# A fused window attention and SwiGLU kernel: a written-out order against an order planned over engines, banks and transfers, with groups of 256 tokens and loads without cast

## The chip, the cores and the metric

One core of one Trainium2 chip. The metric is the device time of one execution in microseconds (us). In the profile, PE is TensorE, DVE is VectorE, ACT is ScalarE, POOL is GpSimd, SP is SyncE, whose work here is to issue transfers.

## The reference

Attention with 4 sink positions and a window of 128 over 4 batches, 8 heads, 768 positions and head size 64, then an RMS norm and a gated feed-forward (512 to 1536 to 512) over the 3072 tokens:

```python
scores = (1.0 / np.sqrt(D)) * np.matmul(q, k.transpose(0, 1, 3, 2))
keep = is_sink | in_window            # pos < 4, or 0 <= row - pos < 128
scores = np.where(keep, scores, -1000000000.0)
a = np.exp(scores - np.max(scores, axis=-1, keepdims=True))
a = a / (np.sum(a, axis=-1, keepdims=True) + 1e-09)
x = np.matmul(a, v)                   # then heads side by side: (3072, 512)
...
xn = x / rms * rms_g
g = xn @ w_gate
silu = g * (1.0 / (1.0 + np.exp(-g)))
out = (silu * (xn @ w_val)) @ w_out
```

Inputs and output are float32; the products are in bfloat16.

## The kernel before

**Attention.** A *visit* is one tile of 128 query positions of one batch for four of the eight heads; there are 48 (`n`: batch, tile, half). It takes three steps. `a_unit` makes the scores of the current and the previous 128 keys in PSUM (L264 for the first tile of a batch, L269 otherwise) in one buffer of two banks, `s2`, of which there is one; lets VectorE overlay the masked part (L275, L281) and the sink scores (L285) and take the row maximum (L288); lets ScalarE take four exponentials (L293); and lets GpSimd pack the sink columns (L299). `b_unit` transposes the probabilities on PE (L308, L312), copies them out on ScalarE (L317) and lets GpSimd select the current and the old part (L325, L329). `c_unit` multiplies by V (L341, L348, L353), divides by the sum (L362, L363) and, after both halves of a tile, squares and sums the rows (L370, L372, L376). `d_unit` scales a tile (L384) and transposes it into `xnt` (L389, L392).

**Each batch's Q and K** are loaded by GpSimd with a cast to bfloat16 (L97), reordered and scaled by VectorE (`order_unit`, L190, L194), transposed on PE (`qk_unit`, L204) and copied to `QT` and `KT` (L210, L214, L218). `sink_unit` (L231, L237, L240) makes the sink scores of a half batch, `vs_unit` (L249) lays out the sink rows of V.

**Feed-forward.** A group is three tiles, 384 tokens (`GROUP = 3`), eight groups. `f_unit` makes gate and value for one of twelve slices of 128 of the 1536 columns (L407), tanh (L412) and two products on VectorE (L414, L418). `o_unit` makes the output of one tile from twelve slices (L424), copies it (L429) and stores it from SyncE (L431).

**Loads.** All but the norm's weight are issued by GpSimd with a cast (L97, L106, L126, L174), in this order: Q and K of batch 0, three tiles of V, the first quarter of the gate and value weights, three tiles of V, the other quarters, the output weights; then Q, K and V of the next batch, from the slots below. `fold_w` (L133, L137) multiplies the norm's weight into the loaded weights in place, on VectorE.

**Order.** Steps of visits are put into slots by hand: slot `n` holds `a_unit(n)`, `c_unit(n - 2)`, `b_unit(n - 1)` and every second time a `d_unit`; a batch's loads, reordering and transposes are put 11 to 1 slots ahead of its first visit. Nine slots run first; then `weave` interleaves six slots with each group's feed-forward by nominal costs. The framework's scheduler makes the final order of each engine from it. PSUM: four banks shared by most steps (`b1`), two for `s2`, two for `pv`.

Of the kernel before, what the change touches and what calls it, by code (L numbers as in the profile page):

```python
# [17 lines left out]
NEG = -1.0e30  # L18


@with_exitstack
def kernel(
# [32 lines left out]
    GROUP = 3  # L55
# [4 lines left out]
    NCH = 4  # L60
    CW = DFF // NCH
    FPC = FTN // NCH
# [4 lines left out]
    stage = ctx.enter_context(tc.tile_pool(name="stage", bufs=8))  # L67
    vpool = ctx.enter_context(tc.tile_pool(name="vpool", bufs=B * NT))
    spool = ctx.enter_context(tc.tile_pool(name="spool", bufs=2))
    ppool = ctx.enter_context(tc.tile_pool(name="ppool", bufs=3))  # L70
    xpool = ctx.enter_context(tc.tile_pool(name="xpool", bufs=3))
    small = ctx.enter_context(tc.tile_pool(name="small", bufs=4))
    xtpool = ctx.enter_context(tc.tile_pool(name="xtpool", bufs=3))
    hpool = ctx.enter_context(tc.tile_pool(name="hpool", bufs=FTN + 3))
    fpool = ctx.enter_context(tc.tile_pool(name="fpool", bufs=3))
    opool = ctx.enter_context(tc.tile_pool(name="opool", bufs=3))
    psum = ctx.enter_context(tc.tile_pool(name="psum", bufs=4, space=bass.MemoryType.PSUM))

    ident = const.tile([P, P], BF16, name="ident")
    nc.gpsimd.memset(ident, 0.0)  # L80
    nc.gpsimd.affine_select(
        out=ident, in_=ident, compare_op=ALU.not_equal, fill=1.0,
        base=0, pattern=[[-1, P]], channel_multiplier=1,
    )
    QT = [const.tile([P, HP, S], BF16, name=f"QT{i}") for i in range(2)]
    KT = [const.tile([P, HP, 2, S], BF16, name=f"KT{i}") for i in range(2)]
    PK = [const.tile([P, P], BF16, name=f"PK{i}") for i in range(3)]
    VS = [const.tile([P, 2, 4 * VW], BF16, name=f"VS{i}") for i in range(2)]

    ST = {}  # L90
    SO = {}
    V16 = {}

    def load_qk(b, half):
        for nm, src in (("q", q), ("k", k)):
            st = stage.tile([P, 4, NT * D], BF16, name=f"{nm}st", tag="st")
            nc.gpsimd.dma_start(  # L97
                out=st,
                in_=src[b, 4 * half:4 * half + 4, :, :].rearrange("h (p j) d -> p h (j d)", j=NT),
            )  # L100
            ST[(nm, b, half)] = st

    def load_v(b, t):
        v16 = vpool.tile([P, H, VW], BF16, name="v16", tag="v16")
        nc.vector.memset(v16[:, :, D:D + 1], 1.0)
        nc.gpsimd.dma_start(  # L106
            out=v16[:, :, 0:D],
            in_=v[b, :, t * P:(t + 1) * P, :].rearrange("h t d -> t h d"),
        )
        V16[(b, t)] = v16  # L110

    load_qk(0, 0)
    load_qk(0, 1)
    for t in range(3):
        load_v(0, t)

# [4 lines left out]
    nc.sync.dma_start(out=rmsg, in_=moe_rms_g.rearrange("(kt p) -> p kt", p=P))  # L121

    def load_w(c):
        cols = slice(c * CW, (c + 1) * CW)
        for dst, src in ((wg_bf, moe_w_gate), (wv_bf, moe_w_val)):
            nc.gpsimd.dma_start(  # L126
                out=dst[:, :, cols], in_=src[:, cols].rearrange("(kt p) f -> p kt f", p=P),
            )

    def fold_w(c):  # L130
        cols = slice(c * CW, (c + 1) * CW)
        for kt in range(KTN):
            nc.vector.tensor_scalar(  # L133
                out=wg_bf[:, kt, cols], in0=wg_bf[:, kt, cols],
                scalar1=rmsg[:, kt:kt + 1], scalar2=None, op0=ALU.mult,
            )
            nc.vector.tensor_scalar(  # L137
                out=wv_bf[:, kt, cols], in0=wv_bf[:, kt, cols],
                scalar1=rmsg[:, kt:kt + 1], scalar2=0.5, op0=ALU.mult, op1=ALU.mult,
            )  # L140


    for i in range(2):
        nc.vector.memset(KT[i][64:128, :, 0, :], 0.0)
        nc.vector.memset(KT[i][0:64, :, 1, :], 0.0)
        nc.gpsimd.memset(VS[i], 0.0)
    for i in range(3):
        nc.gpsimd.memset(PK[i], 0.0)
    negbig = const.tile([P, 1], FP32, name="negbig")
    nc.vector.memset(negbig, NEG)  # L150
    nhalf = const.tile([P, 1], FP32, name="nhalf")
    nc.vector.memset(nhalf, -0.5)

    m_old = const.tile([P, P], I16, name="m_old")
    nc.gpsimd.memset(m_old, 1)
    nc.gpsimd.affine_select(
        out=m_old, in_=m_old, compare_op=ALU.is_gt, fill=0,
        base=0, pattern=[[1, P]], channel_multiplier=-1,
    )

    m_first = const.tile([P, P], I16, name="m_first")
    nc.gpsimd.memset(m_first, 1)
    nc.gpsimd.affine_select(
        out=m_first, in_=m_first, compare_op=ALU.is_gt, fill=0,
        base=0, pattern=[[1, P]], channel_multiplier=-1,
    )
    nc.gpsimd.memset(m_first[:, 0:NS], 0)

    for c in range(NCH):
        load_w(c)  # L170
        if c == 0:
            for t in range(3, NT):
                load_v(0, t)
    nc.gpsimd.dma_start(out=wo_bf, in_=moe_w_out.rearrange("(ft p) d -> p ft d", p=P))  # L174

    SINK = {}
    PT = {}
    PS = {}
    PV = {}
    X16 = {}  # L180
    RR = {}
    XNT = {}

    def order_unit(b, half):

        for nm in ("q", "k"):
            so = stage.tile([P, NT, 4, D], BF16, name=f"{nm}so", tag="so", bufs=4)
            src = ST.pop((nm, b, half)).rearrange("p h (j d) -> p j h d", j=NT)
            if nm == "q":
                nc.vector.tensor_scalar(  # L190
                    out=so, in0=src, scalar1=scale, scalar2=None, op0=ALU.mult,
                )
            else:
                nc.vector.tensor_copy(out=so, in_=src)  # L194
            SO[(nm, b, half)] = so

    def qk_unit(b, hp):
        half, hi = divmod(hp, 2)
        par = b % 2
        for nm in ("q", "k"):  # L200
            pt = psum.tile([P, 512], FP32, name="pqk", tag="b1").bitcast(BF16)
            so = SO[(nm, b, half)]
            for j in range(NT):
                nc.tensor.transpose(  # L204
                    out=pt[:, j * P:(j + 1) * P],
                    in_=so[:, j, 2 * hi:2 * hi + 2, :], identity=ident,
                )
            src = pt[:, 0:NT * P].rearrange("c (j p) -> c p j", j=NT)
            if nm == "q":
                nc.scalar.copy(  # L210
                    out=QT[par][:, hp, :].rearrange("c (p j) -> c p j", j=NT), in_=src,
                )
            else:
                nc.vector.tensor_copy(  # L214
                    out=KT[par][0:64, hp, 0, :].rearrange("c (p j) -> c p j", j=NT),
                    in_=src[0:64],
                )
                nc.scalar.copy(  # L218
                    out=KT[par][64:128, hp, 1, :].rearrange("c (p j) -> c p j", j=NT),
                    in_=src[64:128],  # L220
                )

    def sink_unit(b, half):

        par = b % 2
        ps = psum.tile([P, 512], FP32, name="psk", tag="b1")
        for t in range(1, NT):
            for hi in range(2):
                hp = 2 * half + hi
                c0 = (t * 2 + hi) * 2 * NS  # L230
                nc.tensor.matmul(  # L231
                    out=ps[:, c0:c0 + 2 * NS].rearrange("p (h s) -> p h s", s=NS),
                    lhsT=QT[par][:, hp, t * P:(t + 1) * P], rhs=KT[par][:, hp, :, 0:NS],
                    start=True, stop=True,
                )
        sk = spool.tile([P, NT, 4, NS], FP32, name="sk", tag="sk", bufs=4)
        nc.vector.tensor_copy(  # L237
            out=sk[:, 1:NT], in_=ps[:, 4 * NS:NT * 4 * NS].rearrange("p (t h s) -> p t h s", s=NS, h=4),
        )
        nc.gpsimd.affine_select(  # L240
            out=sk[:, 1], in_=sk[:, 1], compare_op=ALU.is_ge, fill=NEG,
            base=0, pattern=[[0, 4], [-1, NS]], channel_multiplier=1,
        )
        SINK[(b, half)] = sk

    def vs_unit(b):

        for hh in range(4):
            nc.gpsimd.tensor_copy(  # L249
                out=VS[b % 2][32 * hh:32 * hh + NS, :, hh * VW:(hh + 1) * VW],  # L250
                in_=V16[(b, 0)][0:NS, :, :].rearrange("p (x h) c -> p x h c", h=4)[:, :, hh, :],
            )

    def a_unit(n):
        bt, half = divmod(n, 2)
        b, t = divmod(bt, NT)
# [276 lines left out]
```

## Time and profile before

| what | value |
|---|---|
| median of 3 runs | 341.91 us (341.86 to 342.92) |
| profiled execution | 341.6 us, its span 339.9 us |
| busy: PE, DVE, ACT, POOL | 278.8, 237.1, 193.9, 127.8 us |
| mean granted clock of PE | 0.925 |
| loads and stores | 43,197 packets, 20.83 MB |
| HBM read, written | 28.31 MB, 6.29 MB |

Busy time is the union of an engine's instructions. Matmuls are pipelined, so a busy PE need not be PE at its full rate: the time from one matmul's start to the next says more than its duration. In a row of the timeline or of the groups the parts are start, duration, engine, line, operation, `out<-in`, sizes and count; what stands in brackets is the idle time of that engine just before, and what ended it. "DMA" in the slices is the mean busy share of the 16 transfer engines in tenths, PEclk the granted clock in tenths.

### The profile page before, as it was taken

To read this page: it belongs to the slowest core of one execution; us is meant where nothing else is said; L and a number is where in the kernel's file an instruction comes from. 1 tells how busy PE (TensorE), PEld (TensorE's weight loads), DVE (VectorE), ACT (ScalarE), POOL (GpSimd) and SP (SyncE) were. 2 spreads that over 40 slices of the span, in tenths; PEclk is the share of its full clock that TensorE was granted. 3 is DMA by queue.
4 is the path that set the end of the run, shared out by engine and by line. 5 is a ranking of instruction groups with operands and counts; after the bars stand their busy time and mean duration, and the time that the engine had idled before them with its cause. 6 is when DMAs were issued, how large, how long until landed. Compare 5 with 4: busy or idle time off the path is not lost.

```text
span 339.9 us, 5990 instructions
## 1 busy us (share of the span) xinstructions
PE 278.8 (82%) x2129; PEld 166.3 (49%) x2144; DVE 237.1 (70%) x550; ACT 193.9 (57%) x465; POOL 127.8 (38%) x257
## 2 busy tenths in 40 slices
PE   0451257598998889999988999999889999998994
PEld 0430024365654556556645556655446545554651
DVE  7687274678865897589857883898569837872850
ACT  1371145777566677776666677766566666554321
POOL 8972268889421331322413313214021423122000
PEclk9955555789999999999999999999999999999999
DMA  7999999999801000200010001000100010001002
GB/s 106 188 189 204 206 176 64 172 136 183 54 31 64 0 3 2 92 0 4 23 71 1 2 0 64 31 3 3 62 31 2 0 64 32 3 22 72 0 2 93
DMA packets 43197, 20.83 MB, mean 61 GB/s; under 512 B 26272, under 2 KB 40096, under 8 KB 43168
## 3 DMA queue, kind: packets, MB, share of 16 engines
q0 software_dynamic: 39184, 14.16, 36.5%
q1 hardware_dynamic: 3984, 6.30, 4.9%
q8 instruction: 17, 0.28, 0.3%
q14 instruction: 12, 0.10, 0.1%
HBM read 28.31 MB, written 6.29 MB: 102 GB/s over the span
## 4 chain that ended last, share of the span: by engine, by line
PE 40%; ACT 16%; DVE 14%; POOL 14%; issue 8%; DMA 8%; ACTq 0%; POOLq 0%; DVEq 0%
PE po L424 12%; PE pg L407 10%; PE pl L407 9%; ACT ps L293 7%; DMA qst<-in_q_dram 5%; DVE hT L418 4%; POOL v L106 3%; DVE p L414 3%; DVE nmax L288 3%; DMA v<-in_v_dram 2%; ACT pt L317 2%; PE s L269 2%; ACT th L412 2%; POOL rr L376 2%; POOL cur L325 2%
## 5 line engine op out<-in xcount | busy, mean ns | idle before, releaser
L407 PE MATMUL pg<-xnt,wg_bf 128*128 128x384 bf16 x384 | 79.1, 326 | 4.6 <-DVE hT L418 2.7
L407 PE MATMUL pl<-xnt,wv_bf 128*128 128x384 bf16 x384 | 78.0, 326 | 2.4 <-DVE p L414 1.2
L412 ACT ACTIVATE th<-pg 128x384 bf16<-128x384 f32 x96 | 47.6, 498 | 47.8 <-PE pg L407 46.0
L293 ACT ACTIVATE ps<-s,nmax 128x132 bf16<-128x132 f32 (+1 forms) x192 | 55.5, 372 | 33.9 <-DVE nmax L288 28.8
L424 PE MATMUL po<-wo_bf,hT 128*128 128x512 bf16 x273 | 65.1, 379 | 1.7 <-DVE hT L418 0.9
L414 DVE SCALAR_TENSOR_TENSOR p<-th,pg 128x384 bf16<-128x384 bf16 x96 | 52.5, 548 | 16.5 <-ACT th L412 15.5
L418 DVE TENSOR_TENSOR hT<-p,pl 128x384 bf16<-128x384 bf16 x96 | 52.6, 549 | 3.1
L407 PEld LDWEIGHTS <-wv_bf 128*128 128x128 bf16 x384 | 37.5, 98 | 29.6 <-issue 5.1
L407 PEld LDWEIGHTS <-wg_bf 128*128 128x128 bf16 x384 | 35.3, 98 | 25.5 <-issue 7.4
L299 POOL COPY PK<-ps 128x16 bf16<-128x16 bf16 x40 | 8.1, 203 | 97.7 <-ACT ps L293 97.6
L424 PEld LDWEIGHTS <-hT 128*128 128x128 bf16 x288 | 27.2, 98 | 30.6 <-DVE hT L418 0.9
L325 POOL TENSOR_SCALAR_AFFINE_SELECT cur<-pt 128x512 bf16<-128x512 bf16 x40 | 26.0, 651 | 41.2 <-ACT pt L317 40.2
L317 ACT COPY pt<-pp 128x640 bf16<-128x640 bf16 (+1 forms) x48 | 33.0, 687 | 12.7 <-PE pp L312 9.5
L281 DVE COPY_PREDICATED s<-m_old,s 128x512 f32<-128x512 int16 x40 | 27.7, 691 | 17.8 <-PE s L269 17.6
L308 PE MATMUL pp<-ident,ps 128*128 128x128 bf16 x192 | 24.7, 232 | 16.7 <-ACT ps L293 16.5
L288 DVE TENSOR_REDUCE nmax<-s 128x4 f32<-128x528 f32 (+1 forms) x48 | 33.5, 698 | 0.5
L269 PE MATMUL s<-KT,QT 128*128 128x512 bf16 x80 | 27.6, 420 | 4.5 <-ACT ps L293 4.5
L308 PEld LDWEIGHTS <-ps 128*128 128x128 bf16 x192 | 15.6, 102 | 26.1 <-ACT ps L293 19.0
L329 POOL TENSOR_SCALAR_AFFINE_SELECT old<-pt 128x512 bf16<-128x512 bf16 x40 | 26.9, 674 | 0.0
L384 DVE TENSOR_SCALAR xr<-x,rr 128x512 bf16<-128x512 bf16 x24 | 10.4, 432 | 20.1 <-POOL rr L376 20.1
L429 ACT COPY osb<-po 128x512 f32<-128x512 f32 x24 | 14.2, 590 | 18.0 <-PE po L424 18.0
L106 POOL DMA_DIRECT2D v<-in_v_dram x24 | 21.4, 903 | 0.9 <-issue 0.7
(64 smaller groups left out, 365.4 us busy)
## 6 DMA issues: line engine op xcount, KB each, us to landing
out_dram<-osb SPq DMA_DIRECT2D x24, 256.0 KB, 2.0
qst<-in_q_dram POOLq DMA_DIRECT2D x8, 384.0 KB, 6.5
kst<-in_k_dram POOLq DMA_DIRECT2D x8, 384.0 KB, 7.0
v<-in_v_dram POOLq DMA_DIRECT2D x24, 128.0 KB, 5.8
wg_bf<-in_moe_w_gate_dram POOLq DMA_DIRECT2D x4, 384.0 KB, 9.7
wv_bf<-in_moe_w_val_dram POOLq DMA_DIRECT2D x4, 384.0 KB, 10.9
wo_bf<-in_moe_w_out_dram POOLq DMA_DIRECT2D x1, 1536.0 KB, 19.6
rmsg<-in_moe_rms_g_dram SPq DMA_DIRECT2D x1, 2.0 KB, 2.2
```

The costliest lines, as they stand in the source:

```text
L106: nc.gpsimd.dma_start(out=v16[:, :, 0:D], in_=v[b, :, t * P:(t + 1) * P, :].rearrange("h t d -> t h d"),)
L269: nc.tensor.matmul(out=dst, lhsT=lhsT, rhs=KT[par][:, hp, :, (t - 1) * P:(t + 1) * P], start=True, stop=True,)
L288: nc.vector.tensor_reduce(out=nmax, in_=sc[:, :, c0:2 * P], axis=AX.X, op=ALU.max, negate=True,)
L293: nc.scalar.activation(out=ps[:, h, c0 - W0:], in_=sc[:, h, c0:2 * P], func=ACT.Exp, bias=nmax[:, h:h + 1], scale=1.0,)
L308: nc.tensor.transpose(out=pp[:, h * P:(h + 1) * P], in_=ps[:, h, NS:NS + P], identity=ident,)
L317: nc.scalar.copy(out=pt[:, 0:w], in_=pp[:, 0:w])
L325: nc.gpsimd.affine_select(out=cur, in_=pv4, compare_op=ALU.is_ge, fill=0.0, base=0, pattern=[[0, 4], [1, P]], channel_multiplier=-1,)
L407: nc.tensor.matmul(out=dst[:, 0:GN], lhsT=w[:, kt, ft * P:(ft + 1) * P], rhs=xnt[:, kt, :], start=(kt == 0), stop=(kt == KTN - 1),)
L412: nc.scalar.activation(out=th, in_=pg[:, 0:GN], func=ACT.Tanh, scale=0.5)
L414: nc.vector.scalar_tensor_tensor(out=p1, in0=th, scalar=1.0, in1=pg[:, 0:GN], op0=ALU.add, op1=ALU.mult,)
L418: nc.vector.tensor_tensor(out=h_t, in0=p1, in1=pl[:, 0:GN], op=ALU.mult)
L424: nc.tensor.matmul(out=po[:, 0:DM], lhsT=HT[(g, ft)][:, tb * P:(tb + 1) * P], rhs=wo_bf[:, ft, :], start=(ft == 0), stop=(ft == FTN - 1),)
```

## The change

A planner is added. Each step is an operation with an engine, an estimated duration, a delay until its result can be used, what it reads and writes, a rank, and the PSUM banks that it may take. The planner places, again and again, the operation that can start first by its estimates (ties go to the lower rank), with the bank that comes free first. The program is then written in the order of planned starts, and each instruction is tied to the one before it on its engine, so that the framework keeps that order. All tiles are allocated once, with buffers in turn.

Beside this: the scores may take one of two pairs of banks, and all else one of six single banks; a group is two tiles (256 tokens), twelve groups, and `f_unit` makes two slices of 128 columns in one bank of 512; the output product is cut into three parts of four slices; all loads are issued by SyncE without cast into float32 buffers (four for weights, four for Q and K, three for V), weights in smaller tiles; VectorE folds and casts the weights of gate and value (40 operations) and casts the output weights (4); for batch 0 VectorE, for the others GpSimd scales, reorders and casts Q and K; GpSimd casts V; the factor 0.5 moves from the fold to the copy of the output; batch 1's loads stand behind all weights; and visits run eight ahead of the feed-forward.

```diff
+class Plan:
+    def order(self):
...
+            for e, ops in ready.items():
+                for o in ops:
+                    t, c = bank_time(o)
+                    if t is None:
+                        continue
+                    s = max(free.get(e, 0.0), known[o], t)
+                    key = (s, o.rank)
+                    if pick is None or key < pick[0]:
+                        pick = (key, o, c)
...
+            o.start, o.end = s, s + o.lag
+            free[o.engine] = s + o.busy
...
-    GROUP = 3
+    GROUP = 2
...
-    psum = ctx.enter_context(tc.tile_pool(name="psum", bufs=4, space=bass.MemoryType.PSUM))
+    psum = ctx.enter_context(tc.tile_pool(name="psum", bufs=1, space=bass.MemoryType.PSUM))
+    PAIR = [psum.tile([P, 2, 512], FP32, name=f"bank{2 * i}") for i in range(4)]
+    plan = Plan(8)
+    PAIRS_S = [(0, 1), (2, 3)]
+    ONES = [(i,) for i in (7, 6, 5, 4, 3, 2)]
+    def act(el, fn, **kw):
+        return plan.op("ACT", 0.06 + 0.815e-3 * el, fn, lag=0.17, **kw)
+    def dve(us, fn, **kw):
+        return plan.op("DVE", us - 0.06, fn, lag=0.16, **kw)
...
+    ST = ring("st", 4, [P, 4, NT * D], FP32)
+    VST = ring("vst", 3, [P, H, D], FP32)
+    WST = ring("wst", 4, [P, 1536], FP32)
...
-            nc.gpsimd.dma_start(
-                out=st,
+            dma(2.7, lambda src=src, n=n: nc.sync.dma_start(
+                out=ST[n],
                 in_=src[b, 4 * half:4 * half + 4, :, :].rearrange("h (p j) d -> p h (j d)", j=NT),
...
+            def fn(n=n, m=m, nm=nm, eng=nc.vector if b == 0 else nc.gpsimd):
...
+        dma(2.1, lambda: nc.sync.dma_start(
+            out=VST[n], in_=v[b, :, t * P:(t + 1) * P, :].rearrange("h t d -> t h d"),
+        ), writes=[("VST", n)], rank=rank)
+        pool(0.8, lambda: nc.gpsimd.tensor_copy(out=V16[i][:, :, 0:D], in_=VST[n]),
+             reads=[("VST", n)], writes=[("V", i)], rank=rank)
...
+        for kt in range(KTN):
+            dve(0.06 + 0.52e-3 * w, lambda kt=kt: nc.vector.tensor_scalar(
+                out=dst[:, kt, c0:c1], in0=WST[n][:, kt * w:(kt + 1) * w], scalar1=rmsg[:, kt:kt + 1],
+                scalar2=None, op0=ALU.mult,
+            ), reads=[("WST", n), "g"], writes=[(nm, f, kt) for f in range(c0 // P, c1 // P)], rank=rank)
...
+        dve(0.9, lambda: nc.vector.tensor_copy(
+            out=wo_bf[:, f0:f1, :], in_=WST[n].rearrange("p (ft d) -> p ft d", ft=3)),
+            reads=[("WST", n)], writes=[("o", f) for f in range(f0, f1)], rank=rank)
...
+        def mm(bk, w):
+            for i, ft in enumerate(fts):
+                for kt in range(KTN):
+                    nc.tensor.matmul(
+                        out=bank(bk)[:, i * GN:(i + 1) * GN], lhsT=w[:, kt, ft * P:(ft + 1) * P],
+                        rhs=xnt[:, kt, :], start=(kt == 0), stop=(kt == KTN - 1),
+                    )
...
+        act(DM, lambda: nc.scalar.activation(out=OSB[r], in_=bank(bk)[:, 0:DM], func=ACT.Copy, scale=0.5),
+            banks=[bk], after=[o], writes=[("OSB", r)], rank=rank)
...
+            want = (vn - LEAD) * FPG // (2 * GROUP)
+            if want > 0:
+                feed(want + 1)
+            after = [FF[want]] if want > 0 else []
+            visit(vn, float(vn), after)
...
+    done = plan.order()
...
+    for o in sorted(done, key=lambda o: o.start):
+        o.fn()
+    for i in made[seen:] if len(made) > seen else nc.cur_bb.bb.instructions[seen:]:
+        before = last.get(i.engine)
+        if before is not None:
+            tc.add_manual_dep(
+                i, before.name,
+                mybir.DependencyInfo(mybir.DependencyClass.NoSync, mybir.DependencyReason.DATA),
+                reason="the order of the plan",
+            )
+        last[i.engine] = i
```

The order of loads in the plan: Q and K of batch 0; V tiles 0 and 1; gate and value columns 0 to 255; V tile 2; columns 256 to 511; V 3; 512 to 767; V 4; 768 to 1151; V 5; 1152 to 1535; the output weights in four parts; then batches 1 to 3.

## The prediction

> **What bounds the kernel now.** I read the page's slices first, then the stages by window, then the timeline of the first 80 us and of one steady stretch.
>
> ```profile
> span 339.9 us, 5990 instructions
> ...
> PE   0451257598998889999988999999889999998994
> ...
> DVE  7687274678865897589857883898569837872850
> ...
> PEclk9955555789999999999999999999999999999999
> DMA  7999999999801000200010001000100010001002
> GB/s 106 188 189 204 206 176 64 172 136 183 54 31 64 0 3 2 92 0 4 23 71 1 2 0 64 31 3 3 62 31 2 0 64 32 3 22 72 0 2 93
> ```
>
> A slice is 8.5 us. In the first eight PE is mostly idle (and at half its clock in slices 3 to 7) while the DMA engines are full; after that PE is near full to the end. So there are two stages with different limits: a head bound by loads, and a steady part bound by PE. What a stage costs PE I measure by pitch, not busy time, because matmuls overlap. From starts in the steady timeline: 162.5 ns for 384 columns (0.65 us for four), 216 ns for 512 (2.59 for twelve), 56 ns for 128 (0.67 for twelve), 30 ns for the 65-column ones (0.24 for eight). Times the counts of the group view: gate and value 768 x 0.1625 = 124.8; output 288 x 0.216 = 62.2; transposes (192 + 232 + 96) x 0.056 = 29.1; scores 80 x 0.216 + 16 x 0.109 = 19.0; probability times V 352 x 0.030 + 40 x 0.111 = 15.0; sinks 2.0. Sum **252.2 us**.
>
> The first gate matmul starts at 70.6 us. The matmuls recorded before it are worth 13.5 us by these pitches. The last matmul ends at 335.5, so 238.7 us of work took 264.9: **0.90** of full rate. The tail (last copy and store) is 4.4 us.
>
> The head, from the timeline:
>
> ```profile
> 24.77 0.77 POOL L97 DMA_DIRECT2D qst<-in_q_dram  x1
> ...
> 33.25 0.32 DVE L137 TENSOR_SCALAR wv_bf<-wv_bf,rmsg 128x384 bf16<-128x384 bf16 x1 [1.62 <-DMA wv_bf<-in_moe_w_val_dram]
> ...
> 35.07 0.71 DVE L288 TENSOR_REDUCE nmax<-s 128x4 f32<-128x528 f32 x1
> ...
> 35.81 1.15 ACT L293 ACTIVATE ps<-s,nmax 128x132 bf16<-128x132 f32 x4 [6.03 <-DVE nmax L288]
> ...
> 42.79 0.56 DVE L190 TENSOR_SCALAR qso<-qst 128x1536 bf16<-128x1536 bf16 x1 [3.98 <-DMA qst<-in_q_dram]
> ...
> 44.30 1.15 ACT L293 ACTIVATE ps<-s,nmax 128x132 bf16<-128x132 f32 x4 [7.34 <-DVE nmax L288]
> ```
>
> The row maximum of the third visit (L288, 35.07) stands in VectorE's queue behind the folds of all weights, each of which waits for its load; the next one (43.47) stands behind the scaling of batch 1's Q, whose load was issued at 24.77 behind all weights and was usable 18 us later. So attention, ready to run, waits for transfers that it does not need.
>
> The steady part, PE alone:
>
> ```profile
> 176.13 0.59 PE L269 MATMUL s<-KT,QT 128*128 128x512 bf16 x2 [0.95 <-ACT ps L293]
> 177.10 0.30 PE L348 MATMUL pv<-v,pt 128*128 128x65 bf16 x4 [0.37 <-ACT pt L317]
> ...
> 181.41 0.81 PE L407 MATMUL pg<-xnt,wg_bf 128*128 128x384 bf16 x4 [0.78 <-DVE hT L418]
> ```
>
> Scores wait for the only score buffer to be read out, gate matmuls for one of four shared banks. This repeats: two groups (one batch, 63.05 us by pitch) take 70.1 us, from 107.5 to 177.6.
>
> **The change, part by part.**
> PE: 1152 matmuls of 256 columns for 768 of 384. At 256/384 of 160 ns plus the same 2.5 ns they are 109.2 ns each, 125.8 us for 124.8: +1, sum 253.2. More weight loads (98 ns) are no bound: 128-column transposes, each with its own, run at 56 ns.
>
> VectorE: 144 products of 512 elements instead of 192 of 384. A 512-element row is 0.69 (L281), the 384 one 0.548: 99.4 for 105.1, **-5.7**. Twelve reorderings (0.71 mean of L190 and L194) leave: **-8.5**. The folds now read f32: 24 of 256 and 16 of 384 columns, from 10.3 us (fast as now, 0.315 for 384) to 17 (at L281's rate). Casts of the output weights are new: four of 1536 elements, 0.56 (L190) to 2.0 (three times L281) each. In the steady part VectorE gets lighter; it was 74% busy there.
>
> ScalarE: 72 tanh of 512 at 0.612 (L317's 512 row) for 96 at 0.498: -3.5, off the path.
>
> GpSimd: 49 load issues leave, 21.4 (v) + 12.5 (q, k) + 6.3 + 1.9 = 42 us. In come 24 casts of 512 elements (L325: 0.65) and 12 of 1536 (L325's slope of 0.9 ns an element gives 1.6, its rate 1.95): 35 to 39 us; were f32 to cost double, 78. What is queued behind a cast are the selections of a visit, and behind those PE's products. POOL stays near 36% of the span, so I price this at nothing, the cover being the visits planned ahead. Without cover it is the whole 35.
>
> SyncE: 55 loads and 24 stores at 0.33 to 0.42 us, 30 us on an engine with nothing else. With four weight buffers, each weight load from the fifth on waits at the head of this queue for the fold four tiles earlier, and every later load waits behind it; a tile is about 2 us of transfer, so a fold may be some 6 us late before the DMA engines run dry. In the compiled order the first store stands behind loads of batch 3; ScalarE's copy to the three output buffers would wait, and with it a bank. Six banks are shared, so none to 2 us.
>
> VectorE's fast copies lengthen when GpSimd works: xr (L384) runs 336/353/819 ns least, median and most, while L281, which reads PSUM, stays 677/695/697. If all 24 xr paid 0.47, VectorE would lose 11 us; I take 0, since VectorE is not the bound. The Trainium skill, "SBUF — State Buffer", section "SBUF: two separate sides", speaks against the change: GpSimd and a two-port VectorE operation exclude each other for the whole instruction, so casts on both collide. By it with nothing hidden the sum would be 11 us more.
>
> DMA: the rows of queues:
>
> ```profile
> q0 software_dynamic: 39184, 14.16, 36.5%
> q1 hardware_dynamic: 3984, 6.30, 4.9%
> ```
>
> Shares times 16 engines times 339.9 us give 50.7 ns for a packet of q0 (mean 361 B) and 66.9 for one of q1 (1581 B). The loads of batch 0 and all weights are 6 x 1024 + 4 x 512 + 10 x 512 + 12 x 128 = 14,848 packets of 256 B to 2 KB, now on q1: **47 to 62 us**, I take 54, as the sizes lie between. Batch 1's Q comes next instead of ahead of v and beside the weights: 1.2 start + 54 + 2 transfer + 2 landing = 59, plus a GpSimd cast, 61. The skill's "DMA: Bandwidth & Descriptors", section "Specifications", puts HBM at about 358 GB/s a core: 14.2 MB in 40 us as an estimate. No run here shows that; by it the DMA would not bind the head at all.
>
> VectorE in the head: in the compiled order of the changed kernel, one fold of a weight tile stands about after each visit, no longer all before the third. Before its first copy of batch 1's K it has 12 visits' masks and maxima 18.5, eleven divisions 6.6, K copies 3.8, clears 6.1, reorderings 3.0, folds 10.3, output weights 3, seven pairs of products 9.7, xr and sinks 2.7: 64, less 0.07 for each of 125, since independent ones overlap (folds of 0.32 start every 0.23): 55. At the high prices of folds, casts and reorderings it is 72.
>
> So batch 1 can begin at 61 by the loads and at 56 to 73 by VectorE; near the low end, as the folds' nearest row is the fold itself, and with 5 us for VectorE's waits on loads, **T = 66** (60 to 75). By the compiled order PE has then done 12 visits' scores (about 15), 6.5 double units of gate and value (11.4) and an output tile and a half (4.3): 31 us. Left: 253.2 - 31 = 222.
>
> **The sum.** The steady rate is bounded by 0.90 (now) and 0.98 (311.9 to 328, where only gate and value run: 15.8 us of work in 16.1). Two score pairs and six shared banks take away the waits shown above; what is late next is VectorE. In the 36 visits after T it has 54 x 1.38 for products, 36 x 2.16 for visits and 20 for the rest, 172, less 0.06 for each of 310: 153 us. PE has 8.75 groups of 15.7 (96 x 0.1092 + 24 x 0.216) and 50 of attention there: 187. I take 0.95. Span: 66 + 222/0.95 + 4.4 = 304. The profiled execution took 341.6 for a span of 339.9, and the median of the runs is 341.91, so 1.7 to 2 come on top: **306 us**.
>
> **Rivals.**
> 1. Steady rate stays 0.90, because PE queues with a fixed order wait at each product that is a little late. For: that is what bounds it now. Against: the causes were buffers, which change. 66 + 246.7 + 6 = 319.
> 2. It reaches 0.98, T 60: 60 + 226.5 + 6 = 293. For: the stretch at 311.9. Against: VectorE at 82% of PE's work, in an order fixed beforehand.
> 3. Loads no faster than the page's 200 GB/s in the head, now with f32 written: 14.9 MB, 75 us, T 82: 82 + 233.7 + 6 = 322.
> 4. **Slower**: GpSimd's casts become the wait. Place: selections behind a 1536-element cast, PE behind them. Price: at double cost 78 us of casts; if half is exposed, 39 on top of 306 is 345. It decides from 36 us exposed, about 1 us for each of the 36. Against: POOL's cur waits 40 us for ScalarE today, so it is early, not late.
> 5. The change does not do what it says, the compiler reordering the plan. The compiled order shows loads and folds interleaved as planned, so I leave 1 in 100, at about 342.
>
> **Chances.** Forecast (296 to 316) 0.62; rival 1 0.17; rival 2 0.11; rival 3 0.04; rival 4 0.05; rival 5 0.01. A difference below 0.3% can't be told from none in this kernel. Faster 0.94, same 0.01, slower 0.05. The range, from rival 2 to past rival 1 and 3: 291 to 324.
>
> **What would show it.** First gate matmul between 38 and 50 us instead of 70.6; no slice after 66 us with PE below 8; DVE's longest wait on a load under 4 us; pitch-work over time near 0.95 after 66; POOL's selections waiting for ScalarE, not PE for POOL. It is wrong if PE's waits name cur or old, if VectorE's fold of the last tile lies after 66, or if the f32 folds cost over 0.5 us.

## The result, and the profile after

The changed kernel takes **361.55 us** (359.20 to 362.43, four runs) where the kernel before, run beside it, takes 342.07 (341.86 to 342.92): a ratio of 1.055 (1.050 to 1.061). It is 5.5% slower; the forecast was 306 us. The profiled execution took 362.4 us, its span 360.7.

The page of the changed kernel, slices of 9 us:

```profile
span 360.7 us, 6717 instructions
...
PE   0555578787897789899978777899789799998975
...
DVE  7659896976777645685764665776756738836250
...
PEclk9999999999999969899999999999999999999999
DMA  7955854790891591322100001001000000010101
GB/s 243 311 145 151 235 212 134 283 299 16 272 273 56 137 274 31 114 91 78 42 25 36 2 0 50 10 2 60 2 31 29 2 29 31 0 61 0 60 1 58
...
q1 hardware_dynamic: 44272, 34.61, 31.6%
```

The head is no longer a stretch of full DMA engines beside an idle PE: the DMA engines work in bursts and PE works from the second slice on. But the slices behind the head, where the kernel before showed PE at 8 and 9, now mostly show 7 and 8, almost to the end, at full clock but for two slices. No engine took over as the bound: VectorE is less busy than before in most of them.

Measured as in the prediction (matmuls times pitches, which in this trace are 109 ns for 256 columns, 216 for 512 and 56 for 128; T is the start of the first transpose of batch 1, at L359):

| | forecast | changed kernel | costs |
|---|---|---|---|
| work of PE in all | 253.2 us | 252.9 us | 0 |
| T | 66 us | 79.4 us | +13.4 us |
| work done by T | 31 us | 31.1 us | 0 |
| time for the 222 us left | 233.7 us (rate 0.95) | 277.7 us (rate 0.80) | +44.0 us |
| from the last matmul to the end | 4.4 us | 3.6 us | -0.8 us |

The four differences make the whole miss (56.6 us of span). So the question is what holds PE at 0.80. The list of waits of the changed kernel (engine and line, what it waited for; us in all, times, longest) begins with a true use of data, its longest, and has further down lines that no use of data explains:

```profile
POOL cur L497 <- ACT pt L489: 68.1, 32, 3.5
...
DVE p L601 <- PE bank L522: 9.9, 4, 5.4
...
ACT th L597 <- DVE h L604: 6.0, 4, 3.2
...
ACT pt L489 <- DVE h L604: 5.6, 3, 2.6
```

L601 forms the product of tanh and gate; L522 multiplies probabilities by V, for another tile. One of the places in the timeline (start, duration):

```profile
189.89 1.91 PE L586 MATMUL bank<-xnt,wg_bf 128*128 128x256 bf16 x16
...
192.33 1.08 ACT L597 ACTIVATE th<-bank 128x512 bf16<-128x512 f32 x2
192.97 0.27 PE L510 MATMUL bank<-VS,pt 128*128 128x260 bf16 x1 [1.17 <-ACT th L597]
...
193.29 0.19 PE L522 MATMUL bank<-V,old 128*128 128x65 bf16 x1
...
193.59 0.69 DVE L601 SCALAR_TENSOR_TENSOR p<-th,bank 128x512 bf16<-128x512 bf16 x1 [5.37 <-PE bank L522]
...
194.29 0.66 DVE L601 SCALAR_TENSOR_TENSOR p<-th,bank 128x512 bf16<-128x512 bf16 x1
```

At 191.80 PE has finished two banks of gate products. Two tanhs read them (L597), the first until 192.92. PE's next instruction, the sink part of a V product (L510), waits 1.17 us for that first tanh, though it uses nothing of it. Nor can it be writing into one of the gate's banks: L601 reads both again, at 193.59 and 194.29. And the first L601, whose tanh had been there since 192.92, waits until the last V product (L522) is done, 0.67 us longer; the rest of its 5.37 us it would have waited for the tanh anyway, so the sums in the list are more than the price of such waits. Two steps that share neither data nor a bank take turns: the plan has put the two halves of the gate product into banks 4 and 6, and the V product into bank 5, the neighbour of 4.

What they share is a **tile**. The plan hands out single banks, but the program allocates the eight banks as four tiles of two (`PAIR`, in the diff), and the waits that are put into the program are found tile by tile. In the compiled program 369 waits between engines are of this kind: the instruction waited for touches only the other bank of the pair. The plan knows none of them.

### The profile page after: what moved, and what is told of

It is laid out like the page before. It is cut to its first block, busy times and chain, and to the rows that moved or that the text cites. A ratio compares the mean times of both kernels' runs of the same rounds, so it can differ in the third digit from the quotient of the medians.

```text
span 360.7 us, 6717 instructions
## 1 busy us (share of the span) xinstructions
PE 287.2 (80%) x2528; PEld 205.2 (57%) x2528; DVE 235.2 (65%) x488; ACT 192.0 (53%) x441; POOL 116.6 (32%) x244
## 2 busy tenths in 40 slices
DMA packets 44304, 35.03 MB, mean 97 GB/s; under 512 B 26352, under 2 KB 39664, under 8 KB 44272
## 3 DMA queue, kind: packets, MB, share of 16 engines
q1 hardware_dynamic: 44272, 34.61, 31.6%
HBM read 28.31 MB, written 6.29 MB: 96 GB/s over the span
## 5 line engine op out<-in xcount | busy, mean ns | idle before, releaser
L586 PE MATMUL bank<-xnt,wv_bf 128*128 128x256 bf16 x576 | 74.1, 275 | 8.8 <-ACT th L597 2.5
L586 PE MATMUL bank<-xnt,wg_bf 128*128 128x256 bf16 x576 | 74.4, 277 | 7.5 <-DVE x L536 2.1
L601 DVE SCALAR_TENSOR_TENSOR p<-th,bank 128x512 bf16<-128x512 bf16 x72 | 48.7, 682 | 45.9 <-ACT th L597 25.7
L615 PE MATMUL bank<-wo_bf,h 128*128 128x512 bf16 x288 | 72.5, 387 | 7.3 <-DVE h L604 3.2
L586 PEld LDWEIGHTS <-wg_bf 128*128 128x128 bf16 x576 | 56.6, 99 | 20.2 <-issue 10.0
L468 ACT ACTIVATE ps<-bank,nmax 128x132 bf16<-128x132 f32 (+1 forms) x192 | 57.1, 376 | 16.9 <-DVE nmax L464 15.4
L597 ACT ACTIVATE th<-bank 128x512 bf16<-128x512 f32 x72 | 42.5, 601 | 42.6 <-PE bank L586 29.5
L604 DVE TENSOR_TENSOR h<-p,bank 128x512 bf16<-128x512 bf16 x72 | 48.7, 681 | 13.6 <-PE bank L586 8.5
L615 PEld LDWEIGHTS <-h 128*128 128x128 bf16 x288 | 27.7, 99 | 36.8 <-issue 12.6
L497 POOL TENSOR_SCALAR_AFFINE_SELECT cur<-pt 128x512 bf16<-128x512 bf16 x40 | 25.8, 644 | 68.3 <-ACT pt L489 68.1
L489 ACT COPY pt<-bank 128x640 bf16<-128x640 bf16 (+1 forms) x48 | 32.3, 676 | 26.6 <-DVE h L604 5.6
L464 DVE TENSOR_REDUCE nmax<-bank 128x4 f32<-128x528 f32 (+1 forms) x48 | 33.5, 698 | 0.7
L359 PE MATMUL bank<-ident,so 128*128 128x128 bf16 x192 | 16.4, 245 | 10.8 <-DVE so L297 8.8
L374 DVE COPY KT<-bank 64x768 bf16<-64x768 bf16 x16 | 15.0, 946 | 12.9 <-ACT KT L377 9.6
```

The source lines that it names most:

```text
L464: o = dve(0.70, lambda: nc.vector.tensor_reduce(out=nm, in_=sc()[:, :, c0:2 * P], axis=AX.X, op=ALU.max, negate=True,), banks=[sb], after= ...
L468: act(240, lambda h=h: nc.scalar.activation(out=PSM[r3][:, h, c0 - W0:], in_=sc()[:, h, c0:2 * P], func=ACT.Exp, bias=nm[:, h:h + 1], scal ...
L489: act(w * P, lambda: nc.scalar.copy(out=PTT[r3][:, 0:w, :].rearrange("p h c -> p (h c)"), in_=bank(pb).bitcast(BF16)[:, 0:w * P],), banks= ...
L497: pool(0.62, lambda: nc.gpsimd.affine_select(out=cur, in_=PTT[r3][:, 0:4, :], compare_op=ALU.is_ge, fill=0.0, base=0, pattern=[[0, 4], [1, ...
L586: nc.tensor.matmul(out=bank(bk)[:, i * GN:(i + 1) * GN], lhsT=w[:, kt, ft * P:(ft + 1) * P], rhs=xnt[:, kt, :], start=(kt == 0), stop=(kt ...
L597: t = act(512, lambda: nc.scalar.activation(out=TH[r], in_=b3(gb), func=ACT.Tanh, scale=0.5), banks=[gb], after=[o], writes=[("TH", r)], r ...
```

## The experiments

Each line of the table is one kernel, with the time of the kernel before on the same chip (342.07 to 342.45) in the ratio. T and the rate from T to the last matmul are read as above.

| kernel | us | ratio to before | T, us | rate after T |
|---|---|---|---|---|
| changed kernel | 361.55 | 1.055 (1.050 to 1.061) | 79.4 | 0.80 |
| e3, banks 4 to 7 untied | 327.52 | 0.957 (0.952 to 0.961) | 78.3 | 0.91 |
| e2, one pair of score banks, all tied | 352.61 | 1.029 (1.024 to 1.034) | 79.1 | 0.83 |
| e1, as e2, banks 2 to 7 untied | 311.96 | 0.910 (0.907 to 0.913) | 72.6 | 0.95 |
| e9, as e1, plan told measured times | 309.51 | 0.904 (0.901 to 0.906) | 66.6 | 0.97 |
| e10, three banks, tied to none in use | 349.26 | 1.022 (1.017 to 1.027) | 71.4 | 0.84 |
| e11, two pairs for scores only, four untied | 327.82 | 0.959 (0.955 to 0.962) | 75.7 | 0.90 |
| e7, as e1, loads as before | 332.39 | 0.971 (0.968 to 0.973) | 80.6 | 0.98 |
| e8, as e1, K copies on ScalarE | 314.31 | 0.919 (0.916 to 0.922) | 69.4 | 0.93 |
| e4, before with groups of two tiles | 344.28 | 1.005 (1.003 to 1.007) | | |
| e5, before with its four banks tied | 437.70 | 1.279 (1.276 to 1.282) | | |
| e6, control of e5, untied | 343.83 | 1.004 (1.002 to 1.005) | | |

**e3: the changed kernel with banks 4 to 7 as tiles of their own.** Plan, order and banks are those of the changed kernel, instruction by instruction; waits on the neighbour fall from 369 to 130.

```diff
-    PAIR = [psum.tile([P, 2, 512], FP32, name=f"bank{2 * i}") for i in range(4)]
+    PAIR = [psum.tile([P, 2, 512], FP32, name=f"bank{2 * i}") for i in range(2)]
+    ONE = {i: psum.tile([P, 512], FP32, name=f"one{i}") for i in range(4, 8)}
```

> The changed kernel's plan, order and instructions, unaltered; only PSUM banks 4 to 7 become tiles of one bank each instead of two tiles of two banks. Theory P (neighbour banks): the program tracks a two-bank tile as one thing, so 369 of the changed kernel's waits between engines are on an instruction that touches only the other bank of the pair; the split takes that to 130, so most of the loss goes: 318 to 338 us, the steady pitch-work near 0.9. Theory O (a fixed order with estimated durations stalls by itself): the waits are true ones, so 355 to 362 us as the changed kernel. Theory G (256-token groups cost): no change, 358 to 362.

327.52 us, 34.0 less with nothing but the waits changed. That is within theory P's range and far from the others'. The tie is a cause, and the largest found.

**e2 and e1: the same in a plan that allows to untie all.** Scores need two banks side by side, so one tile of two must stay. e2 gives the plan one pair for the scores, with all banks tied (384 neighbour waits); e1 writes the same plan onto one pair and six single tiles (36).

```diff
# e2
-    PAIRS_S = [(0, 1), (2, 3)]
+    PAIRS_S = [(0, 1)]
# e1, beside that
-    PAIR = [psum.tile([P, 2, 512], FP32, name=f"bank{2 * i}") for i in range(4)]
+    PAIR = [psum.tile([P, 2, 512], FP32, name=f"bank{2 * i}") for i in range(1)]
+    ONE = {i: psum.tile([P, 512], FP32, name=f"one{i}") for i in range(2, 8)}
```

> The changed kernel with one pair of banks for the scores instead of two, so a new plan, with the two-bank tiles kept. It is the control of the next run. Theory P: 384 neighbour waits stay, so 355 to 370 us. Theory O: as well 355 to 370, a little more than the changed kernel for the missing score pair.

> The same plan and order as the control with one score pair, but banks 2 to 7 are tiles of one bank each. Theory P: 36 neighbour waits are left, within the scores, so 305 to 330 us, under the split of banks 4 to 7 unless the missing second score pair costs more. Theory O: within 1% of its control.

352.61, somewhat under the 355 to 370 that both theories gave, and 311.96, as theory P had it: 40.7 us for the tie alone. The order of instructions on each engine is the same in both. Against the changed kernel's 361.55, e2 also says that one pair of score banks in place of two, with the plan made anew for it, is 9 us faster. The engines of e2 and then e1 in the same stretches, busy us in 40 (matmul, weight load, VectorE, ScalarE, GpSimd; then granted clock, DMA share, GB/s):

```profile
160.00:200.00 40.00, 37.07 (x329) 26.29 (x328) 27.84 (x59) 24.85 (x60) 13.46 (x31) 1.00 0.13 41
200.00:240.00 40.00, 35.12 (x338) 25.09 (x337) 27.22 (x55) 25.41 (x56) 10.77 (x26) 1.00 0.04 14
240.00:280.00 40.00, 36.54 (x341) 27.82 (x340) 27.84 (x58) 24.52 (x60) 9.50 (x22) 1.00 0.07 28
```

```profile
160.00:200.00 40.00, 39.66 (x399) 30.16 (x397) 31.17 (x66) 29.45 (x68) 12.69 (x29) 1.00 0.07 28
200.00:240.00 40.00, 40.00 (x375) 30.45 (x374) 31.58 (x68) 27.26 (x71) 11.63 (x26) 1.00 0.08 28
240.00:280.00 40.00, 40.00 (x383) 30.59 (x381) 30.64 (x65) 26.29 (x63) 14.30 (x31) 1.00 0.08 28
```

One plan, one order, one clock: e1's PE has no gap left in 80 of 120 us, and what each engine does there is more, not shorter. A PE of 35 to 37 busy us had looked like 0.9 of full; by pitch it is 0.83 for the whole part after T. e1's slices:

```profile
span 309.1 us, 6739 instructions
...
PE   0453669879798999799999999999999999999995
```

**e10: fewer banks, but none tied to another in use.** All tiles are of two banks again, and the plan may use only one of each for all but the scores.

```diff
-    ONES = [(i,) for i in (7, 6, 5, 4, 3, 2)]
+    ONES = [(i,) for i in (7, 5, 3)]
```

> All banks as two-bank tiles again, as in the changed kernel, but for everything other than the scores the plan uses one bank of each tile only, so three banks where the kernel with one pair of score banks (352.61 us) has six; no neighbour is then in use. Theory P (a neighbour's users make each other wait): three banks that nobody shares are better than six that are shared in twos, 320 to 342 us. Rival B (the number of banks decides, and the tie costs little by itself): half the banks, so slower than 352.6, by 360 to 400 us.

349.26: between the two expectations, and outside both. Three banks alone are as good as six that are tied in twos (352.61), so tying takes away all that the second bank of a tile was to give. But the price of having three banks and not six (37.3 us against e1) was more than theory P had set, so how many banks there are decides as well, though not as rival B had it (360 to 400).

**e5 and e6: the same tie put into the kernel before.** Its four shared banks (`b1`) become two tiles of two, handed out in turn; the control gives the same four as single tiles, handed out in turn.

```diff
+    TB = [psum.tile([P, 2, 512], FP32, name=f"tb{i}", tag=f"tb{i}", bufs=1) for i in range(2)]
+    def b1():
+        i = nb[0] % 4
+        nb[0] += 1
+        return TB[i // 2][:, i % 2, :]
...
-        pg = psum.tile([P, 512], FP32, name="pg", tag="b1")
-        pl = psum.tile([P, 512], FP32, name="pl", tag="b1")
+        pg = b1()
+        pl = b1()
```

> The kernel before, with the four shared banks written as two tiles of two banks each, used in turn; its order of steps is still made by the framework, which may move instructions. Theory P (neighbour banks): tying costs here too, 355 to 385 us. Theory O (only a fixed order makes such waits dear, since the framework can move work): 340 to 350 us.

> Control of the tied kernel: the same four banks as four tiles of one bank each, used in turn. Both theories: as the kernel before, 340 to 346 us.

437.70 against 343.83, above both expectations. Where the order comes from the framework's scheduler, the tie costs 94 us, more than in the planned kernel, and PE has gaps from end to end. e5's page:

```profile
span 435.9 us, 6032 instructions
...
PE   1451567667976686768886596768886978785555
```

VectorE's first product now holds up PE's gate and value products: "PE tb L415 <- DVE p L422" stands among e5's waits with 38.3 us in 35 times, among e6's with 0.7 us in 2. The scheduler moves instructions as well, so 94 us is the price of the tie with that reordering, not of the waits alone.

**e4: the group size by itself**, `GROUP = 3` to `GROUP = 2` in the kernel before.

> The kernel before with groups of two tiles (256 tokens, twelve groups) instead of three, nothing else. Theory G: the 256-column products and more group boundaries are what costs, so 352 to 365 us. Theory P and O: PE gains 1 us of pitch, the products on VectorE and ScalarE are now 144 of 256 elements each (more fixed cost, about 20 us more VectorE work), so 342 to 352 us.

344.28, half a per cent slower. The groups of 256 tokens are not where the time went.

**e7: e1 with the loads put back**: casting transfers issued by GpSimd, folds in place in bfloat16, all reordering on VectorE.

```diff
-            dma(2.7, lambda src=src, n=n: nc.sync.dma_start(
+            cast_dma(2.7, lambda src=src, n=n: nc.gpsimd.dma_start(
...
-                out=dst[:, kt, c0:c1], in0=WST[n][:, kt * w:(kt + 1) * w], scalar1=rmsg[:, kt:kt + 1],
+                out=dst[:, kt, c0:c1], in0=dst[:, kt, c0:c1], scalar1=rmsg[:, kt:kt + 1],
```

> The freed plan (banks 2 to 7 as tiles of one bank, one score pair, 311.96 us) with the loads put back: all of them issued by GpSimd with cast to bfloat16, folds in place on bfloat16, Q and K reordered by VectorE, no casts of V. The prediction's step was that the change of loads brings the point where batch 1 begins forward. Theory L+ (loads by SyncE are a gain in the head): 318 to 330 us, the first transposes of batch 1 at 80 or later. Theory L- (the float32 folds at 0.28 us a start instead of 0.23, casts on GpSimd and four staging buffers cost what the faster transfer gives): 303 to 314 us, no difference to speak of or a gain.

332.39, 20.4 us slower than e1 and 2.4 above theory L+'s range. e7's page:

```profile
PE   0000065369889999998999999999999999999995
...
DMA  7999995021965960340245002400101001010101
GB/s 107 188 187 198 206 193 35 2 16 6 146 75 63 175 68 32 50 79 3 18 80 33 33 34 18 81 0 2 65 2 59 7 2 65 0 66 4 63 2 63
```

The first five slices (41 us) give PE nothing. By T, 80.6 us, it has done 12.8 us of work, where e1 by 72.6 has done 31.2. Behind that e7 runs at 0.98, so only the head is worse. But what PE waits for there is no load:

```profile
41.93 0.22 POOL L246 MEMSET ident<- 128x128 bf16 x1
...
42.57 4.86 PE L357 MATMUL one<-ident,so 128*128 128x128 bf16 x48 [42.57 <-POOL ident L247]
```

The transposes need the identity matrix, which GpSimd makes. In e7's plan GpSimd issues its loads first, up to four V tiles of batch 1, and comes to the identity at 41.93; in e1 the first transposes run before 9 us. Batch 1's Q, issued at 28.94, had landed at 42.70, against 65.55 in e1. So the 20.4 us are the price of this order of GpSimd's queue as much as of the loads, and e7 doesn't show what loads without cast are worth. A plan with the identity ahead of the loads was not run.

**e8: both copies of K's transposes on ScalarE.** In e1 as in the changed kernel VectorE copies one half of a K tile out of a bank and ScalarE the other, and they take turns (in the changed kernel VectorE's L374 waits 9.6 us in all for ScalarE's L377).

```diff
-                o = dve(0.95, lambda src=src: nc.vector.tensor_copy(
+                o = act(768, lambda src=src: nc.scalar.copy(
```

> The freed plan with both half copies of K^T on ScalarE instead of one on VectorE and one on ScalarE. Two engines that read one bank are run one after the other by the program, which the plan does not know: VectorE waits 5.9 us in total for ScalarE's copies of K, 1.56 us at a time in the head. If that and VectorE's load hold the head (theory H): batch 1 begins by 68 instead of 72.6 and the kernel takes 303 to 309 us. If the head waits for transfers (theory T): 310 to 314 us.

314.31, slightly slower than e1 (a ratio of 0.919 for 0.910) and at the edge of theory T's range. Batch 1 begins at 69.4, 3.2 us earlier and short of theory H's 68, but the rate after it falls from 0.95 to 0.93. The turns are real; to give ScalarE both copies loses more behind T than it gains before it.

**e9: e1 with the plan told what the traces measured.**

```diff
-                pool(2.0, fn, **kw)
+                pool(1.5, fn, **kw)
...
-            dve(0.06 + 0.52e-3 * w, lambda kt=kt: nc.vector.tensor_scalar(
+            dve(0.13 + 0.82e-3 * w, lambda kt=kt: nc.vector.tensor_scalar(
...
-                ), banks=[bk], after=[tr_op, *o.waits], writes=[("KT2", par, hp)], rank=rank)
+                ), banks=[bk], after=[tr_op, o], writes=[("KT2", par, hp)], rank=rank)
```

V's cast goes from 0.8 to 0.62 in the same way.

> The split kernel (two tied banks for the scores, six banks of their own, 311.96 us) with the plan told four things that the traces measured: that two engines do not copy out of one bank side by side (ScalarE's copy of K^T comes after VectorE's), 0.13 + 0.82 ns per column for a fold of a weight, 1.5 us for a reordering cast on GpSimd, 0.62 us for V's cast. Theory P (the loss was the tied neighbour banks): what is left does not hang on the plan's estimates, so 305 to 313 us, and no step of 10 us. Rival O in its weaker form (a fixed order loses what its estimates get wrong): the head's late folds and the stall between 120 and 140 us go, and the time falls to 295 to 302 us.

309.51: within theory P's range, 2.5 us below e1, and the fastest of all. Batch 1 begins at 66.6 instead of 72.6, but only part of it arrives at the end, because less of the feed-forward is done by then (23.7 us of work against 31.2). A plan's estimates cost single us; a missing resource cost forty.

**e11: two pairs of score banks, used by scores alone, and four single banks.**

```diff
-    PAIRS_S = [(0, 1)]
-    ONES = [(i,) for i in (7, 6, 5, 4, 3, 2)]
+    PAIRS_S = [(0, 1), (2, 3)]
+    ONES = [(i,) for i in (7, 6, 5, 4)]
```

> The split kernel with two pairs of score banks, as the changed kernel plans it, each a two-bank tile that scores alone use, and four banks of their own for all else (the split kernel: one pair and six). It asks whether the split kernel's head, in which batch 0's visits ran in series at some 4.2 us each, was held by its single pair. If so (theory S): batch 1 begins 3 to 6 us before the split kernel's 72.6 us, and the time is 304 to 310 us unless four shared banks take it back. If not: 310 to 318 us, with the loss in the stretch after 140 us, where four banks serve what six did.

327.82, and T at 75.7: neither expectation. Theory S fell, since a second pair doesn't bring batch 1 forward, and four shared banks cost far more than either theory allowed. With only 13 neighbour waits it stands where e3 stands with 130, so what parts e3 from e1 (15.6 us) is most likely how the banks are shared out between scores and the rest, and not the ties that e3 still has. That is read from two kernels with different plans, so it is argued and not shown.

## Why the prediction was wrong, point by point

**The step that failed: "Two score pairs and six shared banks take away the waits shown above", and with it "I take 0.95".** The program had the banks, but not as buffers that come free one by one: each was tied to its neighbour. The measured rate is 0.80, which costs 44.0 us of the 56.6. Untying alone takes the changed kernel to 0.91 (e3). With one score pair it goes from 0.83 to 0.95 (e2 to e1), and 222 us of work take 233.0, against the forecast's 233.7; that the number is met there is no proof of the step, since the second score pair, which was to help, is not in e1. Both kernels that have it are slower than those with one (361.55 and 352.61 tied, e11's 327.82 and e1's 311.96 untied), each with a plan of its own. The bound that I gave the rate, 0.90 to 0.98, was the second half of the mistake: it held only if the change could not add waits at PE, and the line of the diff that allocates `PAIR` showed that it could. Counting by how much the starts of matmuls lie further apart than their pitch, from 80 us to some 15 us before the end, the changed kernel loses 52 us, e2 44, e3 23, e1 9 and e9 4.

**T, 66 us.** 79.4 in the changed kernel, 72.6 in e1, 66.6 in e9 with measured times in the plan. The step that failed here is the one that gave the loads 59 us and the cast 61: it let batch 1's Q follow the other loads at the pace of the transfers, and put the wait of SyncE's queue for the folds at nothing. The trace has:

```profile
63.77 1.40 DVE L330 TENSOR_SCALAR wv_bf<-wst,rmsg 128x384 bf16<-128x384 f32 x4
65.20 0.37 SPq L339 DMA_DIRECT2D wst<-in_moe_w_out_dram  x1
65.62 0.48 SPq L283 DMA_DIRECT2D st<-in_q_dram  x1
...
76.78 1.47 POOL L297 TENSOR_SCALAR so<-st 128x1536 bf16<-128x1536 f32 x1
...
79.39 0.78 PE L359 MATMUL bank<-ident,so 128*128 128x128 bf16 x11
```

The last of these folds (64.76) frees the buffer that the last output weights wait for (65.20), and batch 1's Q stands right behind them: it is issued at 65.62 instead of some 55. It landed at 71.83, and GpSimd came to its cast at 76.78, behind the selections of visits. In e1 the last fold starts at 57.68 and Q is issued at 58.54, in e9 at 52.02 and 52.87; from issue to T it is 13.7 to 14.1 us in all three. So in these kernels T follows the last fold. Of the 13.4 us, 6.8 are the tie and the second score pair together (to e1), and 6 the plan's wrong estimates (to e9). The work done by T, 31 us, was 31.1, and e9's T has less. The first gate matmul came at 51.8 us, outside 38 to 50; in e1 at 46.3.

**PE's cost of the change, +1 us.** Right: 252.9 by the pitches of this trace, for 253.2.

**VectorE, ScalarE, GpSimd.** The prices held: products of 512 at 0.682 and 0.681 (0.69), tanh at 0.601 (0.612), V's cast at 0.614 (0.65), reordering casts at 1.46 to 1.48 (1.6 to 1.95), output weights at 0.95 (0.56 to 2.0). Too low were the folds, near the low end I chose: four of 256 columns take 1.13 us, 0.26 from start to start, and up to 1.96 beside GpSimd; four of 384 take 1.40, 0.33 from start to start, where I took bfloat16's 0.23. All forty take 15.1 us for the 10.3 that I took, within the stated bounds (17).

**GpSimd's casts at nothing (rival 4).** Right: its selections waited 68.1 us for ScalarE (shown above), and the rows in which PE waits for them make 0.3 us, those of its weight loads 3.0. The kernel is slower, but not by this rival. What was at nothing too, and wasn't, is the reverse: batch 1's cast of Q, whose load had landed, stood 5 us in GpSimd's queue behind selections, as part of T.

**Loads.** The transfers were quicker than priced: q1's 31.6% of 16 engines over 360.7 us are 41 ns for each of its 44,272 packets, so the 14,848 packets of the head are, by this mean, an estimated 38 us and not 54. They did not bind the head (the DMA slices fall to 0 in between, and VectorE's list of waits names no load). What held the loads back was their queue: SyncE stood still behind a weight buffer ("SPq L326 <- DVE wg_bf L330") for up to 9.1 us, where I had said that some 6 would do no harm. Whether loads without cast are a gain at all stays open, as e7's head waited for something else.

**Rival 1, fixed order.** It named a rate of 0.90 because an order fixed beforehand waits at each late product. e1 and e9 have a fixed order too and run at 0.95 and 0.97. So a fixed order by itself doesn't hold the rate at 0.90, and e5 shows that the framework's own order doesn't help against the tie.

**The rival that was missing** is one on the slower side at PE itself: banks that the plan counts singly and the program ties. No row of the page before prices it. Of the three signs that I had named as proof of an error, two did not fire: PE hardly waits for the selections, and the last fold of a gate or value weight starts at 64.8, before 66. That second sign was set too late: with some 14 us from that fold to T, T = 66 needs it by 52. The third, folds over 0.5 us, fired for 7 of 40 (0.72 to 0.78; the median is 0.4). They all looked for the faults that I had thought of. What failed plainly were the general ones: PE below 8 in many slices after 66 us, a rate of 0.80, the first gate matmul.

## What to carry to other kernels

Count buffers by what the program's waits are found on, and not by what the chip has: where one tile spans two PSUM banks, each bank's users wait for the neighbour's users, and a planner that doesn't know loses more by it (40.7 us of 352.6) than by four wrong estimates (2.5 us). In a trace it shows as an engine that waits for an instruction that shares no data with it; look for such a pair before blaming order or estimates. Before forecasting that extra buffers take waits away, read their allocation as closely as their number, and leave the bounds of a rate open downwards. And where loads stand in one queue behind few buffers, price them by the step that frees the buffers (here the folds) and not by the transfers alone.

## What the runs showed of the chip

A fold of float32 to bfloat16 on VectorE slows beside GpSimd. In the changed kernel's timeline, four folds each:

```profile
26.04 1.13 DVE L330 TENSOR_SCALAR wg_bf<-wst,rmsg 128x256 bf16<-128x256 f32 x4
...
32.90 1.90 DVE L330 TENSOR_SCALAR wg_bf<-wst,rmsg 128x256 bf16<-128x256 f32 x4
...
41.14 1.13 DVE L330 TENSOR_SCALAR wg_bf<-wst,rmsg 128x256 bf16<-128x256 f32 x4
...
44.10 1.96 DVE L330 TENSOR_SCALAR wv_bf<-wst,rmsg 128x256 bf16<-128x256 f32 x4
```

```profile
33.30 0.70 POOL L497 TENSOR_SCALAR_AFFINE_SELECT cur<-pt 128x512 bf16<-128x512 bf16 x1 [0.70 <-ACT pt L489]
33.96 0.68 POOL L501 TENSOR_SCALAR_AFFINE_SELECT old<-pt 128x512 bf16<-128x512 bf16 x1
```

GpSimd works beside the second and fourth of these (the selections above, then from 43.72 to 46.62 almost without a break) and is idle in the first and the third. Taken one by one, folds of 256 columns last 0.34 to 0.35 us alone, and four of those beside selections 0.72 to 0.73. The Trainium skill, "SBUF — State Buffer", section "SBUF: two separate sides", has GpSimd and a two-port VectorE operation exclude each other for the whole instruction; that a fold is such an operation no run here shows by itself, but the rows agree with it. The slowed folds cost some 2.7 us of the 15.1 in all; how much of that moved T isn't shown.

In these programs VectorE and ScalarE take turns in copying the two halves of K out of one bank (above): one has a wait for the other. The Trainium skill, "PSUM — Partial Sum Buffer", section "PSUM bank collisions raise a hardware error", asks that engines be kept apart by bank and quadrant of 32 partitions. VectorE copies partitions 0 to 63 and ScalarE 64 to 127, so by that rule these turns would not be needed; no run here leaves them out. Nor does the rule reach beyond the bank, and e1, which lets neighbours work side by side, has nothing longer for it in its trace (gate and value matmuls at 274 and 272 ns, 277 and 275 in the changed kernel).

The transfer engines moved 379 GB/s in one 7.7 us slice of e1, 380 in one of e3 and 381 in one of e11 (8.2 us each), where the prediction had cited about 358 as a page's figure. The measurement decides: that figure was no ceiling in such a stretch. With the casting transfers of the kernel before and of e7 no slice is above 206, but the two can't be compared: the queue counts the bfloat16 bytes of those (14.16 MB on q0), half of the 28.31 MB read from HBM.
